# Score products of four levels in 64 by 64 and 64 by 32 tiles of the TensorE array, in a fused linear attention and SiLU MLP kernel

## The chip, the cores and the metric

The kernel runs on one core of one Trainium2 chip. The metric is the device time of one execution in microseconds; the number to beat or lose to is the median of the runs shown below. All data are float32.

## The reference

For each of 4 batches and 8 heads (48 channels, 768 tokens) a state of 48 by 48 is carried through the tokens, then the result feeds a two-layer MLP:

```
for t in range(768):
    cur = einsum('bhd,bhe->bhde', u * k[t], v[t])
    y[t] = einsum('bhd,bhde->bhe', r[t], state + cur)
    state = w[t][..., None] * state + einsum('bhd,bhe->bhde', k[t], v[t])
x = y.transpose(0, 2, 1, 3).reshape(3072, 384)
h = x @ w_in                      # 384 x 2048
out = (h * sigmoid(h)) @ w_out    # 2048 x 384
```

## The kernel before

The tokens are cut into 6 pieces of 128 (L = 128). A **unit** is one piece of two batches (NB = 2), all 8 heads: 12 units, numbered 0 to 11. Heads go in pairs p (NP = 4), the even head of a pair (e = 0) on partitions 0 to 47 and the odd one (e = 1) on 64 to 111.

Inside a unit, y is score times v, where score[key, query] of a head is the product of k, r and all decays between the two tokens. It is built by **levels** l = 0 to 6: level l covers, in blocks of 2c tokens with c = 2^l, the c first tokens as keys and the c last ones as queries. Before level l the tiles tr (queries) and tk (keys) have been multiplied by decay products of 2^l tokens (`grow_queries`, `grow_keys`), so that one matmul of tk and tr gives the wanted scores. The keys of the second batch are stored in reverse order, so that one tile of 128 columns holds the keys of both batches, in blocks that alternate.

`score_products` makes the products of one level. For each p and e it issues one matmul, with 128 keys as columns of the array, 48 channels as rows, and 128 queries streamed (64 of each batch): 8 matmuls a level, into two PSUM tiles sc[0] and sc[1] of 128 by 512 (one for each e, a bank each). Only a part of a product is wanted (half of it on level 6, a quarter on level 5, less below): the rest is between tokens that the level does not want, or between the two batches. `keep_masked` then takes the wanted ones with a masked copy on VectorE (`copy_predicated`, 128 partitions by 512 elements, mask of the level), one for each e, into the tile score. Score is one buffer (NSC = 1); its other elements stay zero from the start.

From unit 2 on (NTOK = 2) levels come two at a time: `prepare` makes the queries of the second level in a second tr tile (VectorE line 737, ScalarE line 739) before the first is used, and `burst` issues the products of both, 16 matmuls in a row: levels 3 and 4, later levels 5 and 6 (unit 2 and 3 have other ways for 1 and 2, units 4 to 11 get those small ones elsewhere). The first level of a burst goes to the PSUM tiles p_sc, the second to p_m (p_o in unit 2); each name has two buffers. `keep_level` does the copies of one level, `go_on` multiplies for the next one (ScalarE line 595, GpSimd line 625, VectorE line 607).

The MLP's matmuls fill the rest of TensorE: `up` (line 941, 128x256, six for each of 8 steps, evicted by the SiLU of ScalarE on line 950 from p_h, two buffers) and `quarter` (line 1007, 128x192). The order on every engine is written by hand: the main loop takes the groups of `mix(i)` for unit i and puts a number of MLP steps of the two units before behind each group. For units 4 to 11:

```
[(burst, i, 3), (keep_level, i, 3), *sum_steps(i, 3, 4), (block_move, i), ...],
[(keep_level, i, 4), (go_on, i, 4)],
[(prepare, i, 5), (reverse_v, i)],
[(block_spread, i), (block_write, i)],
[(burst, i, 5), (keep_level, i, 5), (keep_level, i, 6), (go_on, i, 6)], *end]
```

`end` holds `turn_k` (transposes of keys into p_m, line 781), `y_state` (line 798: 16 matmuls of 48 rows by 48 columns, 128 streamed, one quadrant of the array each) and `y_values` (line 806: score is the streamed operand). Lines in the views: 669 is the matmul of `score_products`, 679 the masked copy, 698 a copy of blocks on ScalarE that units 0 and 1 use for some levels.

Of the kernel before, what the change touches and what calls it, by code (L numbers as in the profile page):

```python
# [38 lines left out]
def kernel(  # L39
# [11 lines left out]
    nc = tc.nc  # L51

    B, H, S, D = r.shape
    DM, DF = moe_w_in.shape
    L = 128
    NL = 7
    NB = 2
    NP = H // 2
    PD = 64
    Q = NB * NP  # L60
    NX = Q + 2 * NP
    X = 0, NP + Q
# [5 lines left out]
    NTOK = 2  # L68
    NPAIR = 4
    FIRST = 3  # L70
# [248 lines left out]
    NSC = 1  # L319
    score = const.tile([128, NSC, 2, Q, L], F32, name="score")  # L320

    masks = {}
    first = {}
    for l in range(NL):
        c, ni = 1 << l, L >> (l + 1)
# [18 lines left out]
    tw, tr, tk, diag, kq, xt = {}, {}, {}, {}, {}, {}  # L344
# [311 lines left out]
        start_keys(i, nc.gpsimd, False)  # L656


    COPIED = (0, 5, 0), (0, 6, 0), (1, 6, 0)

    def score_products(i, l, queries, sc):
        c, ni = 1 << l, L >> (l + 1)

        for p in range(NP):
            for e in range(2):
                rows = slice(PD * e, PD * e + D)

                apart, r_p, s_p = 2 * (NP - p) - 1, queries[rows, p, :], sc[e][:, p, :]
                nc.tensor.matmul(bass.AP(tensor=s_p.tensor, offset=s_p.offset,  # L669
                                         ap=[s_p.ap[0], [apart * L // 2, 2], [1, L // 2]]),  # L670
                                 lhsT=tk[i][rows, X[l % 2] + p, :],
                                 rhs=bass.AP(tensor=r_p.tensor, offset=r_p.offset + c,
                                             ap=[r_p.ap[0], [apart * L, 2], [2 * c, ni], [1, c]]),
                                 start=True, stop=True)

    def keep_masked(i, l, e, sc):
        c, ni = 1 << l, L >> (l + 1)
        dst = score[:, i % NSC, e].rearrange("p (b q) (i s c) -> p b q i s c", b=NB, s=2, c=c)[:, :, :, :, 1, :]
        nc.vector.copy_predicated(out=dst, mask=masks[l][:, :, None].to_broadcast([128, NB, NP, ni, c]),  # L679
                                  data=sc[e].rearrange("p (b q) (i c) -> p b q i c", b=NB, c=c))  # L680

    def scores(i, l, *between):
        c, ni = 1 << l, L >> (l + 1)

        name = "p_h" if i == 0 and l % 2 == 1 else "p_sc"
        sc = [ps.tile([128, Q, L // 2], F32, name=name, bufs=2) for e in range(2)]
        score_products(i, l, tr[i], sc)
        if i < NTOK and l + 2 < NL:
            odd_keys(i, l + 1)

        def keep(e):
            if (i, l, e) in COPIED:

                for b in range(NB):
                    for x in range(ni):
                        first = 2 * x * c if b == 0 else L - (2 * x + 1) * c
                        rows, columns = slice(first, first + c), slice((2 * x + 1) * c, (2 * x + 2) * c)
                        nc.scalar.copy(out=score[rows, i % NSC, e, b * NP:(b + 1) * NP, columns],
                                       in_=sc[e][rows, b * NP:(b + 1) * NP, x * c:(x + 1) * c])
                return  # L700
            keep_masked(i, l, e, sc)
# [39 lines left out]
    made = {}  # L741

    def burst(i, l):

        other = (second[0], "p_o") if i == NTOK else (ps, "p_m")
        for x, (pool, name) in enumerate(((ps, "p_sc"), other)):
            made[i, l + x] = [pool.tile([128, Q, L // 2], F32, name=name, bufs=2) for e in range(2)]
        score_products(i, l, before.pop((i, l)), made[i, l])
        score_products(i, l + 1, tr[i], made[i, l + 1])

    def keep_level(i, l):
        for e in range(2):
            keep_masked(i, l, e, made[i, l])

    def go_on(i, l):

# [5 lines left out]
    apart = {}  # L762
# [116 lines left out]
    def mix(i):  # L879
# [22 lines left out]
        if i < NPAIR:  # L902
            groups = [[*both(turn, i, "w"), (product, i, 0)],
                      [*both(turn, i, "k"), *both(turn, i, "r"), (odd_ones, i)], [(start_levels, i), (prepare_keys, i, 1)],
                      [(prepare, i, 1), *[(product, i, l) for l in range(1, NL)]],
                      [(burst, i, 1), (keep_level, i, 1)],
                      [(keep_level, i, 2), (go_on, i, 2)],
                      [(prepare, i, 3), (reverse_v, i), (bonus, i, 0)],
                      [(burst, i, 3), (keep_level, i, 3), (bonus_sum, i, 0), (bonus, i, 1), (bonus, i, 2)],
                      [(keep_level, i, 4), (go_on, i, 4), (bonus_sum, i, 1), (load_rk, i + 1), (load_u,)],  # L910
                      [(prepare, i, 5), (make_block_mask,), (bonus_spread, i), (bonus_write, i)],
                      [(burst, i, 5), (keep_level, i, 5), (keep_level, i, 6), (go_on, i, 6)], *end]
        else:
            groups = [[], [(odd_keys, i, 2), (grow_keys, i, 2, False), (grow_queries, i, 2), *sum_steps(i, 2)],
                      [(prepare, i, 3), *bonus_steps(i, 6, 7)],
                      [(burst, i, 3), (keep_level, i, 3), *sum_steps(i, 3, 4), (block_move, i), *at(ahead, (load_rk, i + 1))],
# [4 lines that stand above are left out]
# [231 lines left out]
```

## Time and profile before

| what | value |
|---|---|
| median of 3 runs | 625.29 us (623.36 to 625.88) |
| the profiled execution, its own time | 622.72 us |
| span of the profile | 620.9 us (1.8 us lie around it) |
| TensorE (PE) busy | 613.3 us, 99% |
| VectorE (DVE) busy | 441.7 us, 71% |
| ScalarE (ACT) busy | 198.9 us, 32% |
| GpSimd (POOL) busy | 364.9 us, 59% |
| granted TensorE clock | 1.0 |

A row of the profile gives line, engine, operation, the tiles written and read, shape, count, busy time and mean duration. A float32 matmul of the program leaves two MATMUL records and two LDWEIGHTS records (576 matmuls of line 941 are 1152 records). The end of a matmul record is modelled, so the 99% says that the engine always had something in flight, not how fast it went; how fast it goes is seen from the distance between the starts of records. The profiled execution is 0.4% below the median of the runs.

### The profile page before, as it was taken

What the parts mean: (1) busy time and instruction counts of PE and PEld (TensorE: products, weight loads), DVE (VectorE), ACT (ScalarE), POOL (GpSimd) and SP (SyncE); (2) the same over time, 40 slices, a digit from 0 to 9 for tenths busy, and PEclk for the clock granted to TensorE, in tenths of its full rate; (3) what the DMA queues carried; (4) which work ended last, traced back from release to release, by engine and by line L of the source; (5) the groups of instructions that cost most, each with busy time, mean ns of one, the idle gap of its engine ahead of it and who ended that gap; (6) DMA issues with size and microseconds to landing.
All of it is one profiled execution on the core that took longest, in us unless ns stands there. A gap on an engine that the chain in (4) does not pass through costs nothing.

```text
span 620.9 us, 12674 instructions
## 1 busy us (share of the span) xinstructions
PE 613.3 (99%) x4766; PEld 551.7 (89%) x4766; DVE 441.7 (71%) x749; ACT 198.9 (32%) x400; POOL 364.9 (59%) x414
## 2 busy tenths in 40 slices
PE   8999999999999999999999999999999999999997
PEld 8888876799899899899889889889989989989997
DVE  6879779898895695795596697597597597571041
ACT  6798882231330330330331231221222122221110
POOL 6998388566667478577478378378468458400000
PEclk9999999999999999999999999999999999999999
DMA  9966873453443643543543542542452312101000
GB/s 217 305 153 168 154 215 47 77 93 69 99 67 50 133 66 67 111 65 58 112 65 54 120 62 50 119 71 50 109 77 49 73 39 52 35 2 26 26 0 26
DMA packets 203069, 53.28 MB, mean 86 GB/s; under 512 B 186752, under 2 KB 194816, under 8 KB 203008
## 3 DMA queue, kind: packets, MB, share of 16 engines
q1 hardware_dynamic: 201424, 51.88, 41.1%
q10 hardware_dynamic: 1584, 0.59, 0.5%
q8 instruction: 38, 0.62, 0.4%
q14 instruction: 23, 0.19, 0.1%
HBM read 43.21 MB, written 5.24 MB: 78 GB/s over the span
## 4 chain that ended last, share of the span: by engine, by line
PE 91%; DVE 3%; POOL 2%; DMA 1%; ACT 1%; issue 1%; SPq 0%; DVEq 0%; POOLq 0%; ACTq 0%
PE p_h L941 41%; PE p_o L1007 31%; PE p_sc L669 5%; PE p_m L963 3%; PE p_m L806 3%; PE p_m L669 3%; PE p_m L798 2%; PE p_m L781 1%; POOL tk L625 1%; DMA u_bc<-in_u_dram 1%; PE p_sc L833 1%; POOL tk L649 1%; DVE tr L607 0%; PE p_m L857 0%; DVE block_sums L521 0%
## 5 line engine op out<-in xcount | busy, mean ns | idle before, releaser
L941 PE MATMUL p_h<-xt,w_in_sb 128*128 128x256 f32 x1152 | 258.1, 382 | 0.7 <-POOL tk L649 0.7
L941 PEld LDWEIGHTS p_h<-xt,w_in_sb 128*128 128x128 f32 x1152 | 215.9, 190 | 32.6 <-POOL tk L649 0.9
L950 ACT ACTIVATE gt<-p_h 128x512 f32<-128x512 f32 x90 | 53.6, 597 | 250.8 <-PE p_h L941 250.7
L625 POOL TENSOR_TENSOR tk<-tk,tw 128x256 f32<-128x256 f32 x128 | 88.5, 712 | 58.1 <-ACT tk L595 34.6
L1007 PE MATMUL p_o<-own,temps 128*128 128x192 f32 x528 | 88.4, 327 | 1.0 <-DVE temps L1016 1.0
L1007 PEld LDWEIGHTS p_o<-own,temps 128*128 128x128 f32 x528 | 86.0, 190 | 1.7 <-DVE temps L1016 1.6
L1007 PE MATMUL p_o<-w_out_sb,gt 128*128 128x192 f32 x508 | 87.4, 328 | 0.0
L1007 PEld LDWEIGHTS p_o<-w_out_sb,gt 128*128 128x128 f32 x508 | 82.7, 190 | 0.9 <-issue 0.4
L487 POOL TENSOR_TENSOR ruk<-tokens_rk 128x768 f32<-128x768 f32 (+1 forms) x32 | 51.5, 1622 | 44.7 <-DMA tokens_rk<-in_k_dram 23.1
L408 POOL TENSOR_TENSOR tw<-tw 128x256 f32<-128x256 f32 (+6 forms) x83 | 43.9, 529 | 40.9 <-DVE tw L360 37.0
L989 DVE TENSOR_TENSOR temps<-gt 128x256 f32<-128x256 f32 x84 | 54.6, 650 | 18.3 <-ACT gt L950 18.3
L679 DVE COPY_PREDICATED score<-mask,p_sc 128x512 f32<-128x512 int8 x62 | 44.5, 772 | 13.6 <-PE p_sc L669 12.9
L607 DVE TENSOR_TENSOR tr<-tr,tw 128x512 f32<-128x512 f32 x61 | 48.4, 793 | 3.7 <-POOL tk L625 1.1
L595 ACT COPY tk<-tk 128x256 f32<-128x256 f32 x52 | 21.0, 403 | 91.3 <-POOL tk L625 69.6
L1016 DVE TENSOR_TENSOR partial<-p_o,partial 128x192 f32<-128x192 f32 x33 | 11.8, 357 | 41.1 <-PE p_o L1007 40.9
L669 PEld LDWEIGHTS p_sc<-tr,tk 48*128 48x128 f32 x512 | 31.4, 187 | 10.3 <-issue 6.6
L669 PE MATMUL p_sc<-tr,tk 48*128 48x128 f32 x512 | 37.7, 285 | 0.7 <-POOL tk L625 0.6
L1016 DVE TENSOR_TENSOR temps<-p_o,partial 128x192 f32<-128x192 f32 x22 | 7.9, 357 | 32.4 <-PE p_o L1007 22.9
L1007 PE MATMUL p_o<-w_out_sb,temps 128*128 128x192 f32 x176 | 30.4, 326 | 0.0
L1007 PEld LDWEIGHTS p_o<-w_out_sb,temps 128*128 128x128 f32 x176 | 28.9, 190 | 0.0
L737 DVE TENSOR_TENSOR tr<-tr,tw 128x512 f32<-128x512 f32 x21 | 27.8, 1322 | 0.3
L811 ACT COPY yt<-p_m 48x512 f32<-48x512 f32 x40 | 23.2, 581 | 14.9 <-PE p_m L806 5.8
(175 smaller groups left out, 858.9 us busy)
## 6 DMA issues: line engine op xcount, KB each, us to landing
w_out_sb<-in_moe_w_in_dram SPq DMA_DIRECT2D x6, 768.0 KB, 6.7
w_out_sb<-in_moe_w_out_dram SPq DMA_DIRECT2D x4, 768.0 KB, 5.2
own<-in_moe_w_out_dram SPq DMA_DIRECT2D x4, 768.0 KB, 5.2
tokens_rk<-in_r_dram SPq DMA_DIRECT2D x8, 384.0 KB, 4.6
tokens_rk<-in_k_dram SPq DMA_DIRECT2D x8, 384.0 KB, 5.4
tokens_w<-in_w_dram SPq DMA_DIRECT2D x8, 384.0 KB, 6.4
xt<-yt SPq DMA_DIRECT2D x60, 48.0 KB, 2.0
raw<-in_w_dram SPq DMA_DIRECT2D x80, 32.0 KB, 2.3
```

The source lines that it names most:

```text
L408: engine.tensor_tensor(out=up, in0=t[:, :, 0::2], in1=t[:, :, 1::2], op=ALU.mult)
L487: mul = lambda out, one, two: nc.gpsimd.tensor_tensor(out=out, in0=one, in1=two, op=ALU.mult)
L607: nc.vector.tensor_tensor(out=odd, in0=odd, in1=tw[i][l][:, :, 0::2][:, :, :, None].to_broadcast([128, Q, L >> (l + 1), c]), op=ALU.mult)
L625: nc.gpsimd.tensor_tensor(out=out, in0=have, in1=odd_products(i, l, b, *blocks), op=ALU.mult)
L669: nc.tensor.matmul(bass.AP(tensor=s_p.tensor, offset=s_p.offset, ap=[s_p.ap[0], [apart * L // 2, 2], [1, L // 2]]), lhsT=tk[i][rows, X[l % ...
L679: nc.vector.copy_predicated(out=dst, mask=masks[l][:, :, None].to_broadcast([128, NB, NP, ni, c]), data=sc[e].rearrange("p (b q) (i c) -> ...
L737: nc.vector.tensor_tensor(out=new[:, :, :, 1, :], in0=old[:, :, :, 1, :], in1=tw[i][l][:, :, 0::2][:, :, :, None].to_broadcast([128, Q, L ...
L811: nc.scalar.copy(out=yt[i][PD * e:PD * e + D, :, b, :], in_=p_yt[i, e][PD * b:PD * b + D])
L941: nc.tensor.matmul(p_h[:, a, :], lhsT=w_in_sb[:, c, f * 128:(f + 1) * 128], rhs=xt[i][:, c, :], start=(c == 0), stop=(c == KC - 1))
L950: nc.scalar.activation(out=gt[i, m], in_=p_h, func=AF.Silu)
L989: nc.vector.tensor_tensor(out=out, in0=one, in1=two, op=op)
L1007: nc.tensor.matmul(p, lhsT=left(f), rhs=right[:, f, :], start=(f == 0), stop=(f == FH - 1))
```

## The change

From unit 2 on, levels 3 to 6 are computed in small tiles of the array. A smaller part of the pairs of tokens is multiplied that way.

- Levels 3 and 4 (c = 8, 16): for each p, e and each half x of the keys (64 columns), one matmul with 64 queries, 32 of each batch: 16 matmuls of 48 rows by 64 columns, 64 streamed, in place of 8 of 48 by 128, 128 streamed.
- Level 6 (c = 64): the same numbers, each half x belonging to one batch (`corner`).
- Level 5 (c = 32): four parts x of 32 keys, 32 queries each: 32 matmuls of 48 rows by 32 columns, 32 streamed.
- Copies of levels 3 and 4: four masked copies of 64 partitions by 128 elements for each e (on VectorE) in place of one of 128 by 512.
- Copies of level 5: four plain copies of 32 partitions by 128 for each e, all on ScalarE, in place of the masked copy on VectorE.
- Copies of level 6: two plain copies of 64 partitions by 256 for each e: e = 0 on VectorE, e = 1 on ScalarE.

Units 0 and 1, and levels 0 to 2, stay as they are. The order of all other instructions stays the same.

```diff
+    APART = FIRST
+    def dims_of(have, start, *dims):
+        return bass.AP(tensor=have.tensor, offset=have.offset + start, ap=[have.ap[0], *dims])
+    def corner(l, x):
+        return x % 2, x if x % 2 == 0 else (L >> l) - 1 - x
     def score_products(i, l, queries, sc):
         c, ni = 1 << l, L >> (l + 1)
+        if i >= NTOK and l >= APART:
+            for p in range(NP):
+                for x in range(4 if c == 32 else 2):
+                    for e in range(2):
+                        rows = slice(PD * e, PD * e + D)
+                        if c >= 32:
+                            b, first = corner(l, x)
+                            q = (p, 2 * NP - 1 - p)[b]
+                            to, have = sc[e][x * c:(x + 1) * c, q, first // 2 * c:(first // 2 + 1) * c], queries[rows, q, (first + 1) * c:(first + 2) * c]
+                        else:
+                            apart = 2 * (NP - p) - 1
+                            to = dims_of(sc[e][x * 64:(x + 1) * 64, p, :], 32 * x, [apart * L // 2 + 32 - 64 * x, 2], [1, 32])
+                            have = dims_of(queries[rows, p, :], 64 * x + c, [apart * L + 64 - 128 * x, 2], [2 * c, 32 // c], [1, c])
+                        m = 32 if c == 32 else 64
+                        nc.tensor.matmul(to, lhsT=tk[i][rows, X[l % 2] + p, x * m:(x + 1) * m], rhs=have, start=True, stop=True)
+            return
...
     def keep_level(i, l):
+        c = 1 << l
         for e in range(2):
-            keep_masked(i, l, e, made[i, l])
+            if l < APART:
+                keep_masked(i, l, e, made[i, l])
+                continue
+            for x in range(4 if c == 32 else 2):
+                if c >= 32:
+                    b, first = corner(l, x)
+                    (nc.vector.tensor_copy if (l, e) == (NL - 1, 0) else nc.scalar.copy)(
+                        out=score[x * c:(x + 1) * c, i % NSC, e, b * NP:(b + 1) * NP, (first + 1) * c:(first + 2) * c],
+                        in_=made[i, l][e][x * c:(x + 1) * c, b * NP:(b + 1) * NP, first // 2 * c:(first // 2 + 1) * c])
+                    continue
+                rows = slice(x * 64, (x + 1) * 64)
+                for b in range(NB):
+                    half, inner = (x, 1 - x)[b], [1, c]
+                    nc.vector.copy_predicated(
+                        out=dims_of(score[rows, i % NSC, e, b * NP, :], 64 * half + c, [L, NP], [2 * c, 32 // c], inner),
+                        mask=dims_of(masks[l][rows, b], 32 * half, [0, NP], [c, 32 // c], inner),
+                        data=dims_of(made[i, l][e][rows, b * NP, :], 32 * half, [L // 2, NP], [c, 32 // c], inner))
```

## The prediction

> **What bounds the kernel now.** I read the page first, then the chain of waits, then the timeline around one burst, then the records of TensorE one by one. The page gives busy shares:
>
> ```profile
> PE 613.3 (99%) x4766; PEld 551.7 (89%) x4766; DVE 441.7 (71%) x749; ACT 198.9 (32%) x400; POOL 364.9 (59%) x414
> ...
> PE 91%; DVE 3%; POOL 2%; DMA 1%; ACT 1%; issue 1%; SPq 0%; DVEq 0%; POOLq 0%; ACTq 0%
> ```
>
> The second line is the chain that ended last: TensorE is 91% of it, and the rest lies mostly in the first 36.5 us, ahead of the first L941. So what counts is what a burst costs TensorE. The chain of waits between 530 and 560 us (unit 11; columns: start us, us, what) gives it:
>
> ```profile
> 532.40 1.09 PE p_sc L669 x16
> 533.49 0.89 PE p_m L669 x16
> 534.38 13.15 PE p_h L941 x60
> 547.53 1.09 PE p_sc L669 x16
> 548.62 0.89 PE p_m L669 x16
> 549.51 7.97 PE p_h L941 x36
> 557.48 1.02 PE p_m L798 x32
> ```
>
> A burst takes 1.98 us (1.09 + 0.89), and a unit has two. The last line is the key: y_state (L798) also has 16 matmuls, 128 streamed, but as 64 by 64 quadrants; its 32 records take 1.02 us, where 32 records of the burst take 1.98. It is the change's shape already on the chip.
>
> **What sets these times.** Distances between starts of the trace's records:
> - L941, full array, 256 streamed: one record per 216 ns. L1007, 192: per 163.
> - L669, 48 rows by 128 columns, 128 streamed: two (e = 0 and 1, 4 to 7 ns apart) per 111.5.
> - L798, quadrants, 128 streamed: four (7 ns apart) per 109.
> - L833, two halves of 48 columns, 48 streamed: two per 45.
>
> All are 2N/2.4 ns plus 2.5 to 5 (N streamed; two records a matmul). Different tiles run side by side, and only N and the number of tiles matter. A burst also pays on its edges: 0.10 us between its last group and the next kind of tile, and one weight load ahead of its first group (107 ns for 128 columns, 40 for 48).
>
> **What the Trainium skill says.** "TensorEngine Tiling (Array Packing)", Key Properties: tiles work independently, changing the tiling mode drains the array. The trace agrees (109 ns for four; the 0.10 us at edges). Its Instruction Overhead section and "TensorE: Matmul & The Clock Gate", Back-to-back issue gap, speak against the change: about 60 cycles per matmul, or a floor of some 25 ns start to start, so nothing should be cut from a dimension that is already short. The trace has starts 7 ns apart on different tiles, but no long stream denser than L833's 22.5 ns per record, so a floor on a long stream isn't excluded. The tiling page's PSUM Bottleneck says that the copies may become the bound: checked below.
>
> **Part 1, levels 3 and 4 on TensorE.** 2 x 16 matmuls = 64 records in 16 groups of four. A group: 2 x 64 / 2.4 = 53.3, plus 5 as in L833 = 58.3 ns. Burst: weights of 64 columns 53 + 16 x 58.3 + 100 = 1.09 us, for 1.98: **0.89 saved**.
>
> **Part 2, level 5.** 32 matmuls, 64 records, 8 tiles side by side. Streaming needs 8 groups x (26.7 + 5) = 0.25 us. Feeding needs more: the sequencer's waits ahead of L941 (records at 486.731, 486.856, 486.967 and 487.093 us) come 111 ns apart with nothing between and 125.5 with one matmul between, so a matmul is dispatched in 15 ns: 32 x 15 = 0.48 us. It runs some 18 records ahead (its wait for the burst at 485.94 is done at 482.94, 18 records before), which hides part; I take 0.48, bounds 0.25 and 1.6 (64 x 25). **Level 6**: 8 x 58.3 = 0.47. Edges: 0.03 for weights, 0.10 + 0.05 for the new change of tile between 5 and 6, 0.10 at the end. Sum 1.23 us for 1.98: **0.75 saved**.
>
> A unit saves 1.64 us, ten units (2 to 11) **16.4 us**.
>
> **Part 3, copies of levels 3 and 4 (VectorE).** The rows before, from the view of line 679:
>
> ```profile
> L679 DVE COPY_PREDICATED score<-mask,p_sc x62: 690/710/1376, 18.7 to 549.3; 128x512 f32<-128x512 int8 x62
> L679 DVE COPY_PREDICATED score<-mask,p_m x38: 687/712/727, 144.3 to 550.5; 128x512 f32<-128x512 int8 x38
> ```
>
> A pair takes 1.31 us in the timeline, so one more costs 0.60: 512/0.96 = 0.53, and 0.07 fixed. 64 partitions by 128: 0.13 + 0.07 = 0.20 (L521's 128x192 come 0.28 apart, the same rule). Sixteen: 3.2 us for 2.6, 0.6 more; bounds 0.6 and 3.2, the upper with L339's 0.24 x 1.5 each. Cover: behind them are L607 and the second queries (L737, then L739 on ScalarE) for the burst of levels 5 and 6. In unit 10 these are ready at 494.8 (VectorE 493.0), line 625 at 495.6, the burst at 501.07: 5.4 us of slack, of which the shorter first burst takes 0.9. Covered, up to the bound. Not in **unit 2**: L737 ends at 114.76, TensorE is free by 115.2 and starts at 115.46. The copies start no sooner (L437 holds VectorE until 109.31), so this burst stays near 115.6: the 0.9 is lost and 0.2 with it, **1.1 us back**.
>
> **Part 4, copies of levels 5 and 6.** VectorE drops four masked copies (2.6 us) and gets two of 64x256 (0.34 each): 1.9 less, which more than returns part 3. ScalarE gets eight of 32x128 (0.26 by L698) and two of 64x256 (0.37): 2.8 us a unit. Queued behind them there is the SiLU of p_h (L950). In unit 10 the burst starts at 501.07, the SiLU of the step before at 501.18; copies can start near 501.9 and end by 504.8; the next step's p_h is full at 501.07 + 1.23 + 2.6 = 504.9. No loss; if late by 1 us, the other p_h buffer takes 2.6 us more of TensorE work. y_values needs score only at 512.04. turn_k now waits for ScalarE's release of p_m, 5 us later: covered. GpSimd's keys don't wait for copies. DMAs and their queue are not moved.
>
> **Sum.** 16.4 - 1.1 = 15.3 us: 622.72 -> 607.4 for the profiled execution, span 620.9 -> 605.6. The median shown is 625.29, 2.6 above the profiled one; with the same offset 610.0, and I say 609.5, as full side-by-side work on level 5 would give up to 2 us more.
>
> **Rivals.**
> 1. *Level 5 alone hits a floor.* At 25 ns a record it takes 1.6 us; the second burst is 2.35 for 1.98, and a unit saves 0.52: 5.2 - 1.1 = 4.1, time 621. For: the skill's sentence, and a tile of 48 by 32 is nowhere in the trace. Against: the 15 ns dispatch.
> 2. *The floor holds for all small tiles (slower).* If a long stream gives one record per s ns, bursts take 64 s + 0.2 and 96 s + 0.4 us. With 3.96 for both now, break-even is s = 21 ns (20 with unit 2's loss). At 25: 1.8 + 2.8 = 4.6, +0.64 a unit, plus 1.1: 632.8. For: L833's 22.5 is the densest stream seen. Against: that equals 2N/2.4 + 5 for two tiles, so streaming explains it whole.
> 3. *Copies become the bound.* With copies of 0.36 on VectorE (3.2 us more) and some stretched as the L679 of 1376 ns, the slack of 5.4 is gone in some units: half a us in each and 3 in unit 2, some 5 to 8 us: time 615. For: VectorE is 71% busy. Against: VectorE itself waits some 84 us for TensorE (L1016 70.9, L679 12.9), which is room.
> 4. *No change:* another engine paces the units. Then VectorE (34.5 us busy of the 46.8 between 482.5 and 529.3) or GpSimd (29.8) would have to hold TensorE up; TensorE's own waits for them are under 2 us in the whole trace.
>
> **How the numbers follow.** Forecast as summed, with its own range of 604.5 to 613: chance 0.66. Rival 3: 0.13. Rival 1: 0.11. Rival 2: 0.07. Rival 4: 0.03. Predicted 609.5. The range 604.5 to 616 takes in the forecast and rival 3; rivals 1, 2 and 4 (0.21) are mostly left out, and the lower end is level 5 at 0.25 with no loss in unit 2, and a median as near to the profile as before. A difference of 0.5% (3.1 us) is about what a measurement of this kernel can tell from none. Faster by more: forecast, rival 3, most of rival 1: 0.89. Within: 0.04. Slower: 0.07.
>
> **What would show it.** Right: in the chain, level 3 and 4 in about 1.1 us for 64 records, levels 5 and 6 in about 1.2 for 96; groups of four starts per 58 ns; new copies of 0.2 to 0.3 us; L941 and L1007 as before. Part 2 wrong: starts of level 5 20 ns or more apart, or 15 or more on levels 3, 4 and 6. Part 3 wrong: TensorE waiting for L737 ahead of the second burst in units other than 2. Part 4 wrong: L941 waiting for L950 behind bursts. A time over 622 would say that the 7 ns starts of L798 don't hold for short matmuls.

## The result, and the profile after

| | before | after |
|---|---|---|
| median | 624.33 us (623.00 to 625.88, 4 runs) | 615.36 us (613.39 to 617.43, 4 runs) |
| ratio of the medians | | 0.9856, 95% interval 0.9813 to 0.9899 |
| the profiled execution | 622.72 us | 613.39 us |
| span | 620.9 us | 611.6 us |

The change is faster by 9.0 us; 15 were forecast. (Measured again in experiment 5, with more runs of before beside it, it is faster by 7.3.) Line numbers have moved: 686 is the small-tile matmul, 792 its masked copy, 785 its plain copy, 983 `up` (was 941), 992 the SiLU (950), 1049 `quarter` (1007), 1058 its eviction on VectorE (1016), 1031 the sums for it (989), 762 the queries of a burst (737), 840 and 848 y_state and y_values. Lines up to 657 are as before.

The page of the kernel after, busy shares and the engines' shares of the chain that ended last:

```profile
PE 597.8 (98%) x5726; PEld 536.1 (88%) x5726; DVE 441.5 (72%) x849; ACT 227.5 (37%) x500; POOL 360.5 (59%) x414
...
PE 76%; DVE 12%; DMA 4%; POOL 2%; issue 2%; SPq 2%; ACT 1%; DVEq 0%; POOLq 0%; ACTq 0%
```

There are 960 records more (4766 to 5726), and TensorE is busy 15.5 us less, but its share of the chain fell from 91% to 76%, and VectorE and DMA are on it now. The chain of waits in the same unit as in the prediction (start us, us, what):

```profile
524.57 0.62 PE p_sc L686 x32
525.19 0.47 PE p_m L686 x32
525.66 13.15 PE p_h L983 x60
538.81 0.69 PE p_sc L686 x46
539.49 0.67 PE p_m L686 x32
540.16 7.97 PE p_h L983 x36
548.13 1.02 PE p_m L840 x32
```

A burst of levels 3 and 4 is 1.09 us, one of levels 5 and 6 is 1.36 here (1.31 in the units from 6 to 10), both 1.98 before. `up` and y_state take what they took. So TensorE's own part came. What TensorE waits for tells the rest: first the largest row of before that lies past the first 40 us, then the rows of after (us in total, times, longest):

```profile
PE p_o L1007 <- DVE temps L1016: 1.0, 2, 0.7
```

```profile
PE p_o L1049 <- DVE temps L1058: 5.1, 3, 2.7
PE p_m L1084 <- POOL ident masks.py:199: 1.4, 1, 1.4
PE p_o L686 <- DVE tr L762: 1.1, 1, 1.1
PE p_h L983 <- ACT gt L992: 1.0, 1, 1.0
```

The second row is from the start of the program and stands in both kernels. The other three are 7.2 us in five waits, for 1.0 us in two before. By the distances between starts, TensorE's stalls of over 0.3 us grew from 4.2 to 10.7 us: 1.29 us at 114.8 us (L762, unit 2), 1.17 at 160.3 (L992, behind unit 3's second burst), and three times the fourth `quarter`, which waits for VectorE's first eviction: 1.85 at 184.3, 2.88 at 232.7, 0.89 at 512.8.

**The account.** First bursts 10 x 0.89 = 8.9 us, second bursts 10 x 0.66 = 6.6: 15.5 us saved. Stalls 6.5 more. 622.72 - 15.5 + 6.5 = 613.7; the profiled execution took 613.39. So the question for the experiments is what makes these stalls.

### The profile page after: what moved, and what is told of

Same layout as the page of the kernel before. It is cut to its first block, busy times and chain, and to the rows that moved or that the text cites. A ratio compares the mean times of both kernels' runs of the same rounds, so it can differ in the third digit from the quotient of the medians.

```text
span 611.6 us, 14783 instructions
## 1 busy us (share of the span) xinstructions
PE 597.8 (98%) x5726; PEld 536.1 (88%) x5726; DVE 441.5 (72%) x849; ACT 227.5 (37%) x500; POOL 360.5 (59%) x414
## 4 chain that ended last, share of the span: by engine, by line
PE 76%; DVE 12%; DMA 4%; POOL 2%; issue 2%; SPq 2%; ACT 1%; DVEq 0%; POOLq 0%; ACTq 0%
PE p_h L983 33%; PE p_o L1049 29%; DVE temps L1031 4%; PE p_m L848 2%; PE p_sc L686 2%; PE p_sc L694 2%; DVE tr L607 2%; DVE score L792 1%; DMA raw<-in_w_dram 1%; SPq L109 1%; PE p_m L686 1%; PE p_m L1005 1%; DMA raw<-in_k_dram 1%; POOL tk L625 1%; PE p_m L840 1%
## 5 line engine op out<-in xcount | busy, mean ns | idle before, releaser
L992 ACT ACTIVATE gt<-p_h 128x512 f32<-128x512 f32 x90 | 53.6, 596 | 194.1 <-PE p_h L983 193.9
L625 POOL TENSOR_TENSOR tk<-tk,tw 128x256 f32<-128x256 f32 x128 | 89.9, 723 | 48.5 <-issue 22.9
L1049 PE MATMUL p_o<-own,temps 128*128 128x192 f32 x528 | 88.9, 327 | 5.1 <-DVE temps L1058 5.1
L1049 PEld LDWEIGHTS p_o<-own,temps 128*128 128x128 f32 x528 | 85.9, 190 | 6.4 <-DVE temps L1058 6.0
L1049 PE MATMUL p_o<-w_out_sb,gt 128*128 128x192 f32 x508 | 87.4, 328 | 0.0
L1049 PEld LDWEIGHTS p_o<-w_out_sb,gt 128*128 128x128 f32 x508 | 82.7, 190 | 0.9 <-issue 0.4
L487 POOL TENSOR_TENSOR ruk<-tokens_rk 128x768 f32<-128x768 f32 (+1 forms) x32 | 46.8, 1474 | 54.0 <-DMA tokens_rk<-in_k_dram 37.0
L1031 DVE TENSOR_TENSOR temps<-gt 128x256 f32<-128x256 f32 x84 | 57.5, 684 | 19.8 <-ACT gt L992 19.8
L607 DVE TENSOR_TENSOR tr<-tr,tw 128x512 f32<-128x512 f32 x61 | 53.8, 882 | 4.2 <-POOL tk L625 1.0
L1058 DVE TENSOR_TENSOR partial<-p_o,partial 128x192 f32<-128x192 f32 x33 | 11.8, 357 | 35.2 <-PE p_o L1049 34.9
L1031 DVE TENSOR_TENSOR temps<-temps,gt 128x256 f32<-128x256 f32 x43 | 31.4, 729 | 1.5
L1058 DVE TENSOR_TENSOR temps<-p_o,partial 128x192 f32<-128x192 f32 x22 | 7.9, 358 | 32.4 <-PE p_o L1049 22.9
L1049 PE MATMUL p_o<-w_out_sb,temps 128*128 128x192 f32 x176 | 30.4, 326 | 0.0
L487 POOL TENSOR_TENSOR spare<-tokens_rk 128x384 f32<-128x384 f32 (+1 forms) x16 | 29.0, 1810 | 0.0
L1049 PEld LDWEIGHTS p_o<-w_out_sb,temps 128*128 128x128 f32 x176 | 28.9, 190 | 0.0
L634 POOL TENSOR_TENSOR tk<-tk,tw 128x256 f32<-128x256 f32 x32 | 26.2, 837 | 0.0
L521 DVE TENSOR_REDUCE block_sums<-ruk 128x4 f32<-128x192 f32 (+1 forms) x48 | 24.0, 540 | 2.7 <-POOL ruk L487 2.7
```

Of the source, the lines that this page charges most:

```text
L487: mul = lambda out, one, two: nc.gpsimd.tensor_tensor(out=out, in0=one, in1=two, op=ALU.mult)
L521: add = lambda out, have: nc.vector.tensor_reduce(out=out, in_=have, axis=mybir.AxisListType.X, op=ALU.add)
L607: nc.vector.tensor_tensor(out=odd, in0=odd, in1=tw[i][l][:, :, 0::2][:, :, :, None].to_broadcast([128, Q, L >> (l + 1), c]), op=ALU.mult)
L625: nc.gpsimd.tensor_tensor(out=out, in0=have, in1=odd_products(i, l, b, *blocks), op=ALU.mult)
L634: nc.gpsimd.tensor_tensor(out=have, in0=have, in1=odd_products(i, l, b, [2, NP * ni]), op=ALU.mult)
L992: nc.scalar.activation(out=gt[i, m], in_=p_h, func=AF.Silu)
```

## The experiments

Theory T at the start: each burst saves what it lost in length, and stalls take back what VectorE, later by its eight small copies ahead of the block sums, does not deliver in time. Rival P: each part is worth what the prediction's sum says. Rival C: what is missing is the price of the copies alone, some 6 us. Before ran beside every set (622.45 to 622.62 us). In the texts on record a wait ahead of a unit's first burst is sometimes counted to the unit before; the times in us say which is meant.

**1 and 2. Each half alone.**

```diff
-        if i >= NTOK and l >= APART:
+        if i >= NTOK and APART <= l < 5:      # e_34; keep_level likewise
```
```diff
-    APART = FIRST
+    APART = 5                                 # e_56
```

> Small tiles and their copies on levels 3 and 4 alone; levels 5 and 6 as before. Theory T (TensorE sum, plus a VectorE stretch that sets when unit 4's quarters can go on): each of ten bursts of levels 3 and 4 takes 1.09 us instead of 1.98, 8.9 us in all, but VectorE gets 0.77 us more ahead of the block sums and keeps its four masked copies on levels 5 and 6, so in unit 4 nothing is left of what was gained by then (2.7 us and 0.8 more) and later units give 0.9 each at best: about 619 to 621. Rival P (only TensorE's time counts): 615.5. Rival C (the new copies cost time wherever they are): 622 or more.

Measured: 617.25 us (616.46 to 619.82), ratio 0.992, interval 0.9901 to 0.994; between the numbers of T and of P.

> Small tiles and their copies on levels 5 and 6 alone; levels 3 and 4 as before. Theory T: ten bursts of levels 5 and 6 at 1.31 instead of 1.98 give 6.7 us; VectorE loses 1.8 us of copies per unit and the block sums aren't late, so of the stalls only the one behind unit 3's second burst (SiLU late, 1.1 us) stays: about 618.5. Rival P: 617.6. Rival C: 621 or more.

Measured: 617.65 us (616.89 to 620.19), ratio 0.9925, interval 0.9906 to 0.9944: the number of P, not of T. Bursts save 8.9 and 6.7 us; stalls grow by about 3 and 2. With levels 3 and 4 alone the saving of 0.89 a unit is seen whole from unit 5 on (period 47.98 to 47.09 us), and so is that of levels 5 and 6 (47.31). Nearly all that is lost is lost ahead of 235 us in both. T's cause fails in the second: levels 3 and 4 have their old copies there, so nothing is later ahead of the block sums, and still TensorE waits 2.4 us for L1058 at 232.3 us; the wait for the SiLU that T expected did not come.

**3. The copies alone**, with the old matmuls.

```diff
-        if i >= NTOK and l >= APART:
+        if False:
```

> The matmuls of before with the new copies on levels 3 to 6. Theory T: TensorE isn't shortened, so nothing waits for the copies; VectorE's longest stretch is 1 us shorter: 623.5 to 624.5, no difference from before. Rival C: the copies cost some 6 us: 630. Rival P: 624.3.

Measured: 624.10 us (622.87 to 627.70), ratio 1.0026, interval 1.0014 to 1.0038. The copies cost 1.6 us by themselves, little but clear of noise (T expected nothing, C 6), and the period of the late units stays 47.98. So C falls: they aren't the bound, and the 6.5 us need the faster TensorE too.

**4. Block sums ahead of the small copies.** The small masked copies stand on VectorE ahead of L521, whose sums go out by kept, come back, and feed L557.

```diff
-[(burst, i, 3), (keep_level, i, 3), *sum_steps(i, 3, 4), (block_move, i), ...],
+[(burst, i, 3), *sum_steps(i, 3, 4), (block_move, i), (keep_level, i, 3), ...],
```

> The changed kernel with the block sums (line 521) and the move of them put ahead of level 3's copies in the groups of units 4 to 11. Theory T: the masked block write (line 557) comes some 2 us sooner, the stalls of 2.7 us in unit 4 and 0.9 us in unit 11 go: about 3.5 us less than the changed kernel, 611 to 612. Rival P and a theory of late loads: as the changed kernel, 615.4.

Measured: 613.25 us (612.38 to 615.01), ratio 0.9847, interval 0.9829 to 0.9865. The stall at 512 us has gone; that at 233 us, which T had going too, has not (3.3 us). The changed kernel's interval (next) overlaps this one, so by itself it isn't shown as a gain.

**5. The changed kernel again**, as the measure for 6 to 8.

> The changed kernel once more, as the measure for the other three runs beside it: 613.4 to 615.4 us, a ratio of 0.983 to 0.988 to the kernel before; stalls of TensorE behind L1058 of about 1.9 us near 184 us, 2.9 us near 232 us and 0.9 us near 512 us, the gain at the first quarter of unit 5 (277 us) about 1.2 us.

Measured: 615.14 us (614.25 to 616.93), ratio 0.9872, interval 0.9856 to 0.9888; stalls 1.86, 3.49 and 0.99 us at the three places.

**6. Small tiles from unit 5 on.**

```diff
-        if i >= NTOK and l >= APART:
+        if i >= 5 and l >= APART:             # keep_level likewise
```

> Small tiles and their copies only from unit 5 on; units 2, 3 and 4 as in the kernel before. Theory floor: up to the first quarter of unit 5 the kernel is paced by loads and by VectorE's stretch ahead of L1058, and three units' shorter bursts bring 1.2 us there instead of 4.7; so leaving them away costs at most 1.2 us: 613.5 to 615.8 us, not more than 1.2 us above the changed kernel beside it; the SiLU wait of 1.1 us in unit 3 and the L762 wait in unit 2 gone. Rival, that each unit gives the same: 3 of 10 units are gone, so three tenths of the gain of 9 us, 2.7 us above the changed kernel or, if each was worth its 1.55 us, 4.7 us above.

Measured: 613.70 us (613.28 to 615.94), ratio 0.9861, interval 0.9843 to 0.9879. Leaving three units' bursts long costs nothing; the median is even 1.4 us below the changed kernel. The rival, 2.7 to 4.7 us more, falls. Units 2 to 4 bring nothing: the waits for L762 and L992 are gone, that at 186 us is 0.92 again. But 2.3 us came at 235.3 (the kernel is as before up to there; the load of k landed 7.0 us after its issue instead of 5.4) and 1.6 at 470, in a unit where nothing had been late in the changed kernel. So VectorE's lateness isn't bound to the early units. That nothing is gained ahead of 235 us can be read directly: unit 5's first burst starts at 246.35 us in the profile after and at 246.04 in that of before. Which wait paces these units no run took apart.

**7. The eviction earlier.** L521's first two sums (1.48 us) behind the first L1058 instead of ahead of it.

```diff
-                *at(ahead, *sum_steps(i + 1, 0, 1), *bonus_steps(i + 1, 4, 5)), (move_x, i)]]
+                (move_x, i)]]
...
-            groups = [[], [(odd_keys, i, 2), ...
+            groups = [[], [*sum_steps(i, 0, 1), *bonus_steps(i, 4, 5), (odd_keys, i, 2), ...
-        room = (1, 1, 0, 2, 1, 1, 1, 1, 1, 2, 2, 1, 1, 0) if i < NPAIR else (3, 2, 2, 1, 1, 1, 2, 1, 1, 1, 0)
+        room = (1, 1, 0, 2, 1, 1, 1, 1, 1, 2, 2, 1, 1, 0) if i < NPAIR else (2, 3, 2, 1, 1, 1, 2, 1, 1, 1, 0)
```

> The changed kernel with the first two block sums (L521, 0.94 and 0.54 us) and the two bonus steps beside them put behind the second quarter's eviction L1058 instead of ahead of it, in units 4 to 11; TensorE's order is unchanged. If the stalls of L1049 come from VectorE's queue ahead of L1058, that eviction comes 1.48 us earlier: the wait near 232 us falls from 2.9 to about 1.4 us, that near 512 us from 0.9 to 0, and that of unit 3 (184 us, not touched) stays at 1.9; 1 to 2.5 us below the changed kernel beside it. Rival, that the pace there is VectorE's whole stretch from 222 us on and not the eviction alone: the stall goes on to the next wait of the same unit (L762 or the keys' L607 behind it) and the time stays within 0.5 us.

Measured: 621.39 us (620.17 to 623.58), ratio 0.9982, interval 0.997 to 0.9994: 6 us above the changed kernel. The list of unit 4 is touched as well, so the wait at 184 us changed too, unlike what was expected. TensorE's waits:

```profile
PE p_o L1049 <- DVE partial L1058: 7.5, 8, 1.9
...
PE p_o L1049 <- DVE temps L1058: 0.8, 2, 0.4
```

The wait for the first eviction (temps) is nearly gone, as the theory has it, and a wait for the second (partial) has taken its place, in all eight units: it now stands behind L521, the keys' L607 and four more sums. The order before had been right; what is late is VectorE's whole stretch. That the wait moves on is what the rival said, but it moved to another place than the rival named, and neither text had a loss of 6 us.

**8. Level 5 in the form of level 4** (below: the quad form). Twice the columns, half the instructions; the other half of what is multiplied isn't used.

```diff
-                for x in range(4 if c == 32 else 2):
+                for x in range(2):
...
-                        if c >= 32:
+                        if c > 32:
...
-                        m = 32 if c == 32 else 64
+                        m = 64
```

> The changed kernel with level 5 in the form of levels 3 and 4 (64 keys by 64 queries, 16 matmuls instead of 32), its copies unchanged, so half of what it multiplies is not used. Theory dispatch: the 32 small matmuls of level 5 take 0.69 us because TensorE's sequencer gives out one in 16.5 ns, not because of their columns; 16 take about 0.47 us as level 4 does, the burst of levels 5 and 6 falls from 1.31 to about 1.09 us, and ten units save 2.2 us: 1.5 to 2 us below the changed kernel beside it. Rival, that columns or the copies behind the burst set the time: within 0.5 us, or slower, as twice the columns are multiplied.

Measured: 617.46 us (616.23 to 618.04), ratio 0.9911, interval 0.9897 to 0.9925. The burst did what dispatch says: 1.09 us for 1.31 in every undisturbed unit, 0.515 us for level 5 instead of 0.69. Yet the kernel is 2.3 us **slower** than with 32 matmuls: 2.2 us less work for TensorE, and stalls of 3.49 us at 232.7, 1.86 at 424 and 1.35 at 517. Less work on the bound engine made the kernel slower. VectorE's timeline ahead of the stall at 424 us shows how (start us, us, engine, line; the bracket is idle time before and what ended it):

```profile
404.35 0.86 DVE L785 COPY score<-p_m 64x256 f32<-64x256 f32 x2 [0.47 <-PE p_m L686]
405.24 1.81 DVE L607 TENSOR_TENSOR tr<-tr,tw 128x512 f32<-128x512 f32 x1
406.97 2.03 DVE L1031 TENSOR_TENSOR temps<-gt 128x256 f32<-128x256 f32 x1
409.04 1.11 DVE L1031 TENSOR_TENSOR temps<-temps,gt 128x256 f32<-128x256 f32 x1
410.07 1.23 DVE L1031 TENSOR_TENSOR temps<-gt 128x256 f32<-128x256 f32 x1
411.23 0.41 DVE L1031 TENSOR_TENSOR temps<-gt,temps 128x256 f32<-128x256 f32 x1
...
426.04 0.36 DVE L1058 TENSOR_TENSOR temps<-p_o,partial 128x192 f32<-128x192 f32 x1
```

From the copy of level 6 to L1058 VectorE has no gap: 21.7 us in a row. L607 takes 1.81 and three of the sums 1.1 to 2.0, where the sum of 411.23 takes 0.41. GpSimd in that stretch:

```profile
404.69 1.81 POOL L487 TENSOR_TENSOR ruk<-tokens_rk 128x768 f32<-128x768 f32 x1 [6.50 <-DMA tokens_rk<-in_k_dram]
406.57 2.14 POOL L487 TENSOR_TENSOR ruk<-ruk,u_bc 128x768 f32<-128x768 f32 x1
408.67 1.19 POOL L487 TENSOR_TENSOR spare<-tokens_rk 128x384 f32<-128x384 f32 x1
409.94 1.08 POOL L487 TENSOR_TENSOR tokens_rk<-tokens_rk,tokens_w 128x384 f32<-128x384 f32 x1
```

L487 waited 6.5 us for a load, and runs exactly beside the long instructions; when it ends (411.0), the next sum takes 0.41. The Trainium skill says in "Trainium Architecture — The Big Picture", What this means for kernel authors, that VectorE and GpSimd share a port pair of SBUF and take it in turns. These rows agree: two and a half to five times the duration beside L487, and each of the four ends 0.3 to 0.6 us behind the L487 instruction that it ran beside. And the load? SP's queue, which it stands in:

```profile
393.60 0.33 SPq L540 DMA_DIRECT2D kept<-block_sums  x1
397.28 1.01 SPq L543 DMA_DIRECT2D spare<-kept  x2
398.38 0.66 SPq L139 DMA_DIRECT2D tokens_rk<-in_r_dram  x1
399.09 0.59 SPq L139 DMA_DIRECT2D tokens_rk<-in_k_dram  x1
```

It is issued behind kept (which waits for L521) and behind the readback of kept (which waits for kept to land). And kept itself is slow here, 3.7 us from issue to landing. In the stretch from 386 to 408 us, the queue that fetches instructions (packets, MB, share; its one packet starts at 395.21) and the row of kept (issues, KB each, us to landing):

```profile
q8 instruction: 1, 0.02, 0.2%
kept<-block_sums SPq DMA_DIRECT2D x1, 64.0 KB, 3.7
```

Beside it a unit of the kernel after that has no stall; the readback follows 1.6 us behind kept:

```profile
390.44 0.33 SPq L540 DMA_DIRECT2D kept<-block_sums  x1
392.01 1.00 SPq L543 DMA_DIRECT2D spare<-kept  x2
```

**The new theory: a late load.** kept goes out at a fixed time behind the first burst, and what follows from it is not TensorE's. TensorE's second burst comes earlier by what both bursts save. In units 5 to 9 kept is issued 4.2 us after the first burst's start before the change and 4.7 after it, and the last record of the second burst starts 16.9 and 15.4 us after that same start: seen from the second burst, kept, the load and L487 are 2.0 us later, 1.5 by the shorter bursts and 0.5 by the copies. How much L1058 is late can then be read in all traces from where L487 starts (the burst ends where the next kind of record starts; all times in us):

| trace, place | L487's start, from the end of the second burst | L607 behind the burst | stall of `quarter` |
|---|---|---|---|
| before, units 5 to 9 | -4.2 to -3.7 us | 0.67 to 0.88 us | none |
| after, units 5 to 9 | -2.2 to -1.6 | 1.2 to 1.6 | 0 to 0.1 us |
| before, 234.8 us | -1.2 | 1.4 | 0.5 |
| after, 512.8 us | -0.3 | 1.1 | 0.9 |
| from unit 5, 470 us | +0.2 | 1.6 | 1.6 |
| quad form, 424 us | +0.5 | 1.8 | 1.9 |
| after, 232.7 us | +1.5 | 2.1 | 2.9 |
| quad form, 232.7 us | +2.4 | 2.4 | 3.5 |

The slack that all this eats is small: in before's units 5 to 9 the eviction L1016 is over 1.0 to 1.2 us ahead of the time at which the fourth `quarter` needs its bank, in after's 0.25 to 0.7 us.

These 2 us use most of the slack up, but past 235 us they don't make a stall of over 0.5 us by themselves; the rest is the slow kept. In five traces with this order of the sums (after, its repeat, e_34, from unit 5, the quad form) kept is issued 35 times in units 5 to 11. In 29 it lands after 1.5 to 1.9 us, and `quarter` loses 0.4 us at most. In six a packet of 16 KB of the instruction queue starts 0.9 to 1.7 us behind kept and takes 0.9 to 1.5 us; the last eight of kept's 128 packets start when it is done, kept lands after 3.0 to 3.7 us, and these are the units of all the stalls of over 0.5 us there: 512.8 us in after and its like in the repeat, 470 from unit 5, 424 and 517 in the quad form (in e_34 the stall is 0.2 us). So the profile of the quad form lost more: it has two such units, each profile of the changed kernel one. This is read from the traces; no run moved these packets.

**9, 10 and 11. The load earlier**, in two ways, and with the rest put together.

```diff
# e_quad5_sf: level 5 as in 8, order as in 4
# e_quad5_rk: level 5 as in 8, and
-[(burst, i, 3), (keep_level, i, 3), *sum_steps(i, 3, 4), (block_move, i), *at(ahead, (load_rk, i + 1))],
+[*at(ahead, (load_rk, i + 1)), (burst, i, 3), (keep_level, i, 3), *sum_steps(i, 3, 4), (block_move, i)],
# e_best_sf: small tiles from unit 5 on as in 6, level 5 as in 8, order as in 4
```

> Level 5 in 64 by 64 tiles, and only the three loads of the next unit's tokens moved ahead of kept on SP's queue in units 4 to 11; the order of TensorE, VectorE, ScalarE and GpSimd is unchanged. Theory late load: the loads are issued about 7 us earlier (near 391 us instead of 398.4 us in unit 8), L487 starts near 398 us, at -5 us or before, and the stalls of units 8 and 11 go: 613.5 to 614.5 us. Rival: the 1.1 MB of the tokens now stand ahead of the 64 KB of kept in the transfer engines; kept lands up to 4 us later, L551 and L557 come late, the copy L785 behind them and with it L1058: no gain, 617 us or more.

Measured: 615.44 us (613.50 to 616.41), ratio 0.9871, interval 0.9843 to 0.9899. The stalls at 424 and 517 us are gone. The unit that had the one at 424 us, VectorE first:

```profile
406.89 0.86 DVE L785 COPY score<-p_m 64x256 f32<-64x256 f32 x2
407.77 0.69 DVE L607 TENSOR_TENSOR tr<-tr,tw 128x512 f32<-128x512 f32 x1
408.38 0.42 DVE L1031 TENSOR_TENSOR temps<-gt 128x256 f32<-128x256 f32 x1
```

```profile
398.73 1.81 POOL L487 TENSOR_TENSOR ruk<-tokens_rk 128x768 f32<-128x768 f32 x1
```

With only the place of three loads on SP changed, L487 starts 6.1 us ahead of the burst's end, L607 takes 0.69 for 1.81 and the sums 0.42 for up to 2.03. So the late start of L487 is what stretches them. The rival's price is there too: kept now stands behind 1.1 MB, L551 waits 5.9 us for it, the copy L785 is late, and in unit 4, where tokens_rk comes free only at 206 us, kept is held until 208.3 us and TensorE loses 5.9 us behind its second burst. So 2 us of the 3.5 expected came.

> Level 5 in 64 by 64 tiles, and the last two block sums (L521) with the transfer kept<-block_sums behind them ahead of the copies of level 3 in units 4 to 11. Theory late load: the load of tokens_rk, queued on SP behind kept and its readback, lands late, so GpSimd's L487 starts late; where it starts later than about 1.6 us before the second burst's end it runs beside VectorE's L607 and first sums L1031 and stretches them, and L1058 comes late (over the units of all traces so far: start at -0.2 us, stall 1.0; +0.5 us, 1.9; +1.5 us, 2.9; +2.4 us, 3.5; before -1.6 us none to 0.1). kept goes 2.5 us earlier here, L487 starts at -3 us or before in units 5 to 11, the stalls of 1.9 us (unit 8) and 1.3 us (unit 11) of the quad form go: 613.5 to 614.5 us, unit period 46.2. Rival, that 46.2 us is shorter than VectorE's own stretch allows, whatever GpSimd does: the lateness adds up over units and a stall of 1 to 2 us turns up again; 616 to 617.5 us.

Measured: 614.14 us (610.60 to 614.97), ratio 0.9845, interval 0.9816 to 0.9873. L487 starts at -2.4 us or before from unit 5 on (-3 was expected; kept took 3.1 and 3.5 us to land in units 5 and 6), no `quarter` stalls there, and the period is 46.2 us. The rival, that VectorE can't hold this period, falls. 3.5 us stay at 232 us.

> Small tiles from unit 5 on only, level 5 in 64 by 64 tiles, block sums and kept ahead of the copies of level 3. From the run from unit 5 on (613.7 us): 7 times 0.22 us for level 5, and its stall of 1.6 us in unit 10 gone by the earlier load: 610.3 to 611.3 us. Rival, that VectorE's stretch sets the period: 613 us or more.

Measured: 610.02 us (609.51 to 610.27), ratio 0.9784, interval 0.9759 to 0.9809. Below both kernels, and the account closes: 7 units x (0.89 + 0.89) = 12.5 us, and 622.55 - 610.02 = 12.5. TensorE's share of the chain is 91% again, and its waits are those of before:

```profile
PE p_m L1084 <- POOL ident masks.py:199: 1.4, 1, 1.4
PE p_o L1049 <- DVE temps L1058: 1.2, 2, 0.8
PE p_h L983 <- POOL tk L649: 0.7, 1, 0.7
```

**A second price of a stall: the clock.** In the kernel of 8 TensorE's granted clock is not 1.0. Stretches of 2 us (PE, PEld, DVE, ACT and POOL busy, PEclk, DMA share, GB/s):

```profile
234.00:236.00 2.00, 0.00 (x0) 0.00 (x0) 1.97 (x4) 0.41 (x1) 0.50 (x2) 0.82 0.24 66
236.00:238.00 2.00, 1.65 (x5) 1.65 (x6) 1.16 (x3) 0.00 (x0) 2.00 (x3) 0.50 0.21 57
...
240.00:242.00 2.00, 2.00 (x8) 2.00 (x8) 0.12 (x1) 0.39 (x2) 1.92 (x4) 0.50 0.38 63
242.00:244.00 2.00, 2.00 (x14) 2.00 (x13) 0.24 (x1) 0.54 (x2) 2.00 (x3) 0.98 0.40 50
```

TensorE is idle for 3.5 us, then gets half its clock for some 6 us, where the records of L1049 start 320 ns apart instead of 163. That is 3 us more for this one stall, and the account shows it: 622.72 - 17.9 + 9.9 of stalls = 614.7, and this execution took 617.9. The Trainium skill has the rule in "TensorE: Matmul & The Clock Gate", HAM oscillation: no idle gaps of TensorE over some 3.4 us. Here it is worse and less sure: in the profiles of experiments 4 and 7 the clock was 0.50 for 3.4 us after stalls of 1.6 and 2.1 us, while the profiled executions of after (2.9 us) and of e_quad5_sf (3.5 us) kept 1.0.

**12. The stall filled.** Transposes of the identity, whose result nobody reads, ahead of the fourth `quarter`, in the kernel e_quad5_sf.

```diff
+        if which == 3 and i in (1, 2):
+            beat((12, 26)[i - 1])
         p = second[0].tile([128, DH], F32, name="p_o", bufs=2)
```

> The kernel with level 5 in 64 by 64 tiles and the block sums first (614.1 us, the granted clock 0.994 to 0.997 in five of its six executions and 1.0 in the one of 610.6 us), with TensorE kept at work through two waits for L1058: 12 and 26 transposes of the identity (0.109 us each, 1.3 and 2.8 us), whose result nobody reads, ahead of the fourth quarter in units 3 and 4. Theory idle: TensorE's wait of 3.5 us in unit 4 lowers the granted clock to 0.50 for some 6 us after it, which costs 3 us more; with the wait filled the clock stays at 1.0 and most executions take 610.5 to 611.5 us. Rival, that the clock falls for another reason: about 614 us with a clock of 0.994 as before, or more, as the transposes are extra work.

Measured: 614.23 us (612.76 to 615.30), ratio 0.9858, interval 0.9837 to 0.9878. This decides nothing: the transposes stand at the wrong place. The 26 filled the stall at 184 us, and that at 235 us stayed (3.5 us), with the clock at 0.50 for 3.4 us behind it. Whether a filled wait keeps the clock up is open. The clock goes with such stalls in most kernels (e_best_sf, longest stall past the first 40 us 1.0 us: 1.0 in all five executions; the quad form: 0.991 to 0.997 in all five), but not in all: before, whose profile has no stall of over 0.9 us there, had 0.996 and 0.997 in two of 11 executions. No run isolates it.

## Why the prediction was right, and where it was not

- **Part 1 held to the number.** 1.09 us forecast, 1.09 in all ten units. Groups of four records start every 58 to 59 ns, 58.3 forecast; that is under 15 ns a record in a long stream. So rivals 1 and 2 did not come. They took the floor of some 25 ns that the Trainium skill gives in "TensorE: Matmul & The Clock Gate", Back-to-back issue gap, for a floor between any two records; records on four tiles side by side go below it. Whether one tile alone keeps to it, no run here shows.
- **Part 2 was mis-sized by 0.08 us.** 1.31 us measured, 1.23 forecast. The cause was right (16 matmuls in place of 32 took 0.22 off, experiment 8), the term was not: once the sequencer's lead is used up, level 5's records come in pairs every 16.5 ns, and level 5 takes 0.69 us with its edges where the sum has 0.66 (0.48 + 0.03 + 0.15), level 6 0.63 where it has 0.57. Over ten units 0.9 us.
- **Part 3 failed in its list of what stands behind the copies.** A small copy is 0.26 us in a row of eight (2.07 us), not 0.20, so two levels cost 1.5 us a unit, not 0.6: the fixed part, 0.07 by a fit to two larger shapes of two operations, was too low for this one. The forecast's bounds held that, and L762 was covered, in all units but 2, as it said. But behind the copies on VectorE stand L521, kept, and by SP's queue the next unit's load, and GpSimd's L487 behind that. "DMAs and their queue are not moved" was true of the order and missed the time: 0.5 us later from the copies, 1.5 from the second burst coming earlier; a slow kept added 2 in the units that stalled past 235 us.
- **Part 4's "No loss" failed once**, in unit 3. ScalarE waits there for a transfer (L577, from own_sums), not for its copies, and holds the SiLU back:

```profile
160.15 0.84 ACT L577 COPY both_b<-diag 32x16 f32<-32x16 f32 x4 [1.03 <-DMA diag<-own_sums]
160.90 1.06 ACT L992 ACTIVATE gt<-p_h 128x512 f32<-128x512 f32 x2
```

  The shorter second burst alone doesn't do it: e_56 has it too, and no such wait. With levels 3 and 4 small as well, the second burst starts 0.9 us earlier, and the last of own_sums (L441 on VectorE, behind the small copies) comes later, 7.7 us after the first burst's start instead of 7.1 in e_56. Together TensorE lost 1.2. Elsewhere the eight copies on ScalarE cost nothing.
- **The sum had 1.1 us of loss, and there were 6.5.** This is the step that failed: "VectorE itself waits some 84 us for TensorE (L1016 70.9, L679 12.9), which is room". Most of the 70.9 lay behind the first eviction of a unit, where VectorE waits for one quarter after the other. Ahead of it there were 1.0 to 1.2 us, and below zero at two places already (TensorE's waits of 0.7 and 0.3). A sum of waits over the span isn't the slack of the next deadline. The larger part of the loss lies ahead of 235 us: for units 2 to 4 the forecast counted 3 x 1.64 - 1.1 = 3.8 us, and unit 5 starts no earlier than before.
- **The rivals.** The time came out as rival 3 has it (615), by another way: the copies alone cost 1.6 us, the wait was L1058 and not L762, and past 235 us it comes of a load that is late, seen from TensorE. The measured 615.36 lies outside the forecast's own range (604.5 to 613), and inside the stated one only because that took in rival 3, whose way to this number (5.4 us of slack ahead of L762 used up by copies) was not taken. What TensorE does was understood; that the total fell in the range was luck. Up to 235 us the time is as rival 4 has it, no change (experiment 6), and not after.
- **The median** has a term that no sum had: in two of after's four runs the mean granted clock was 0.997, and they are the two slowest (615.82 and 617.43).

## What to carry to other kernels

When the bound engine gets faster inside a period, list for every other engine and queue the next time at which the bound engine needs it, and take each slack there; a total of idle time says nothing. What comes a fixed time after an early step (a load queued behind a store and its readback) gets later, seen from the bound engine, by exactly what that engine saved. Leave it slack for a slow transfer too: here some landed 2 us late, and only where the slack was used up did that cost anything. Apply a speed-up only where the bound engine sets the pace: left out of the three units ahead of 235 us, given the same 64 by 64 form on level 5, and with the load earlier, the change brings 12.5 us instead of 7 to 9.

## What the runs showed of the hardware

- Four tiles of 48 by 64 with 64 columns streamed start as a group every 58 to 59 ns; 48 by 32 tiles with 32 streamed come down to one matmul in 16.5 ns, so for these halving the number of instructions is worth more than halving the columns: level 5 takes 0.69 us as 32 of these and 0.515 as 16 of 48 by 64.
- A masked copy of 64 by 128 from PSUM takes 0.26 us in a row of like ones, one of 128 by 512 0.65: an eighth of the elements for two fifths of the time.
- L607 and the sums L1031 (VectorE, two inputs in SBUF) take 0.69 and 0.42 us alone and up to 2.4 and 2.0 beside GpSimd's L487.
- A transfer of 64 KB in 128 packets lands after 1.5 us; where a packet of 16 KB of the instruction queue starts 0.9 to 1.7 us behind its issue, its last eight packets wait for that one and it lands after 3.0 to 3.7 us.
- After TensorE stalls of 1.6 to 5.9 us the granted clock was 0.50 for 3.4 or 6.8 us in six of the fourteen profiles, and stalls of 2.9 and 3.5 us in two others left it at 1.0: a stall can cost twice its length.
